# A decode kernel whose value, key and output-weight loads move from SyncE's DMA queue to GpSimd's, each engine's share in one packet

## The chip, the cores and the metric

The kernel runs on one core of a Trainium2 chip. The metric is the device time of one execution, in microseconds (us). A core has TensorE (PE), VectorE (DVE), ScalarE (ACT), GpSimd (POOL) and SyncE (SP), which run their own instruction streams and meet at semaphores, and 16 DMA engines that move data between the chip's memory (HBM) and the core's on-chip memory of 128 partitions. A DMA is issued by one of the engines, goes into that engine's queue, and is spread over the 16 DMA engines; each of them adds 1 to the DMA's semaphore when its share has landed, so a finished DMA counts 16.

## What is computed

One token of a gated mix of two parts. Nearly all the work is in the first, attention over a cache of 65536 positions with 8 key/value heads of size 256 and 16 query heads:

```python
q = (x @ wq).reshape(B, Sq, Hq, Dh)           # 1 token, Hq = 16, Dh = 256
k = jnp.repeat(k_cache, 2, axis=1)            # k_cache, v_cache: 1 x 8 x 65536 x 256, bf16
scores = jnp.einsum("bhqd,bhkd->bhqk", q, k) * (Dh ** -0.5)
o = jnp.einsum("bhqk,bhkd->bhqd", softmax(scores), v)
a = o.reshape(B, Sq, Hq * Dh) @ wo
out = g * a + (1 - g) * b                     # g = sigmoid(sum(x * gate_w)); b: a small MLP of x
```

The two caches are 256 MB each; the weights W_q and W_o are under 4 MB each. The second part, b, is a LayerNorm and an MLP along the token axis, done on DVE and ACT in small pieces beside the attention.

## The kernel before

The cache of one head is read in 4 pieces, so that there are 32 *bodies* (j = 0 to 31) of 16384 positions, each with 8 MB of keys and 8 MB of values. A body is a tile of 128 partitions with 128 positions each, 64 KB per partition. Keys go to `kring` (L107), which has room for one and a half bodies; values go to `vbuf` (L109), which has room for one. `vbuf` holds W_q and the small inputs at the start.

PE works through a body in 8 *chunks* of 16 positions per partition. For each it transposes the keys through the identity (`transposes`, L344 to L370, the matmul of L359), DVE and ACT copy the result to `ktT` (L675, L820), and PE multiplies it with the query (`scores`, L380). Chunks 0 to 3 use positions 64 to 127 of the body, chunks 4 to 7 positions 0 to 63. After the last chunk the running maximum is updated (`maxima`), ACT makes the weights `pT` (L807), and PE multiplies them with the values (`values`, L411 within `some`). For bodies 0 and 1 the values follow the keys of the same body. From body 3 on (`LEAD` = 2) PE first does the keys of body j and then the values of body j - 1. At the end of a head, PE projects the result with a piece of W_o (`wo_rows`, L466 to L472, the wait in L574).

All large loads are issued by SP, in the order of its program (L257 to L323):

- The first piece of W_o (L263), W_q in two parts (L264, L266), and the keys of body 0 in two halves, positions 64 to 127 first (L272), then 0 to 63 (L273). None of them waits.
- `load_v(j)` (L275 to L285) loads the values of body j: for j = 0 after W_q has been used (`s_q`, `s_hb`), otherwise after the values of body j - 1 have been used (`sem_pv`). At the first body of a head it also loads the next piece of W_o.
- The loop of L287 to L308 loads the keys of body j after PE has transposed chunk 3 of body j - 1 (L294; the semaphore of bank 3 counts chunks), then the values of body j, for j of 2 and less, or of body j - 1. Body 2 comes in two halves, body 3 in a half and two quarters, body 31 in two halves.
- The values of body 31 come in five pieces (L311 to L316), the last piece of W_o in two (L317 to L320), and at the end SP stores the output (L322).

All these loads of whole key bodies count on one semaphore, `sem_k`, for which PE waits before chunk 0 (L346) with 16 x (j + 1). The second halves have their own semaphores, for which PE waits before chunk 4 (L347 to L351). The two quarters of body 3 have two semaphores of their own; POOL waits for both and then adds 16 to `sem_k` (L335 to L337). This, and the making of an identity matrix and of ones at the start (L327 to L334), is all that POOL does. ACT issues six small loads at the start (L780 to L785).

Of the kernel before, what the change touches and what calls it, by code (L numbers as in the profile page):

```python
# [7 lines left out]
AF = mybir.ActivationFunctionType  # L8
ALU = mybir.AluOpType
AX = mybir.AxisListType  # L10


def bass_gated_mix__gqa_block_cached__mixer_token_mlp__decode_kernel(
# [17 lines left out]
    H = A_k_cache.shape[1]  # L31
    T = A_k_cache.shape[2]
    DH = A_k_cache.shape[3]
    DM = A_x.shape[-1]
    HQ = A_wq.shape[1] // DH
    REP = HQ // H
# [9 lines left out]
    DC = 4  # L46
    NB = NT // 4
    NCPH = T // CH
    NC = H * NCPH
    BODY = 2 * DC  # L50
    NV = BODY * NT
    NP = NC // BODY
    PPH = NCPH // BODY
# [10 lines left out]
    LEAD = 2  # L64
    assert LEAD % 2 == 0 and 1 < LEAD < PPH
    NLATE = 112
    NRING = 72
    pieces = [(0, NRING), (NRING, 96), (96, NLATE), (NLATE, 124), (124, NV)]
# [16 lines left out]
    HV = NV // 2  # L85
# [11 lines left out]
    with ctx:  # L97
# [6 lines left out]
        def new_sem(name):  # L104
            return ctx.enter_context(nc.semaphore(name))

        kring = sb([P, NV + HV, DH], bf16, "kring")  # L107
        kring_f = kring.bitcast(f32)
        vbuf = sb([P, NV, DH], bf16, "vbuf")  # L109
# [10 lines left out]
        wo_sb = sb([P, REP, 2 * DM], bf16, "wo_sb")  # L120


        wo_rows = wo_sb[:, :, :].rearrange("p h n -> p (h n)")
# [73 lines left out]

        sem_k = new_sem("sem_k")
        sem_kb = new_sem("sem_kb")
        sem_kc = [new_sem("sem_kc%d" % i) for i in range(3)]  # L200
        sem_kq = [new_sem("sem_kq%d" % i) for i in range(2)]
        sem_v = new_sem("sem_v")
        sem_vp = [new_sem("semvp%d" % i) for i in range(len(pieces))]
# [3 lines left out]
        sem_wo = new_sem("sem_wo")  # L207
# [6 lines left out]
        sem_pv = new_sem("sem_pv")  # L214
# [37 lines left out]
        def src(cache, j, n0=0, n1=NV):  # L252
            g, m = divmod(j, PPH)
            s = cache[0, g, m * BODY * CH:(m + 1) * BODY * CH, :].rearrange("(p n) d -> p n d", p=P)
            return s[:, n0:n1, :].rearrange("p n d -> p (n d)")

        @block.sync  # L257
        def _(eng):
            def load_wo(g):
                w = A_wo[g * REP * DH:(g + 1) * REP * DH, :]  # L260
                eng.dma_start(wo_rows, w.rearrange("(p i) n -> p (i n)", i=2 * REP)).then_inc(sem_wo, 16)

            load_wo(0)  # L263
            eng.dma_start(wq_a.rearrange("p j n -> p (j n)"),  # L264
                          A_wq[0:WF * P, :].rearrange("(p j) n -> p (j n)", p=P)).then_inc(sem_wq, 16)
            eng.dma_start(wq_b, A_wq[WF * P:DM, :].rearrange("r (a n) -> (r a) n", a=2)  # L266
                          ).then_inc(sem_wq, 16)
            def load(dst, cache, j, n0, n1, at, sem):
                eng.dma_start(dst[:, at + n0:at + n1, :].rearrange("p n d -> p (n d)"), src(cache, j, n0, n1)
                              ).then_inc(sem, 16)  # L270

            load(kring, A_k_cache, 0, HV, NV, 0, sem_k)  # L272
            load(kring, A_k_cache, 0, 0, HV, 0, sem_kb)  # L273

            def load_v(j):  # L275
                if j == 0:
                    eng.wait_ge(s_q, 1)
                    eng.wait_ge(s_hb, 1)
                else:
                    eng.wait_ge(sem_pv, j)  # L280
                load(vbuf, A_v_cache, j, 0, NV, 0, sem_v)
                g, m = divmod(j, PPH)
                if m == 0 and 1 <= g < H - 1:
                    eng.wait_ge(s_proj, g)
                    load_wo(g)  # L285

            for j in range(NP):  # L287
                if j == LEAD + 1:
                    eng.wait_ge(sem_tr[NB - 1], BODY * LEAD)
                    load(kring, A_k_cache, j, HV, NV, HV, sem_kc[1])  # L290
                    eng.wait_ge(sem_tr[NB - 1], BODY * LEAD + DC // 2)
                    load(kring, A_k_cache, j, 0, HV // 2, HV, sem_kq[0])
                if j >= 1:
                    eng.wait_ge(sem_tr[NB - 1], BODY * (j - 1) + DC)  # L294
                if j == LEAD:
                    load(kring, A_k_cache, j, HV, NV, 0, sem_k)
                    load(kring, A_k_cache, j, 0, HV, 0, sem_kc[0])
                elif j == LEAD + 1:
                    load(kring, A_k_cache, j, HV // 2, HV, HV, sem_kq[1])
                elif j == NP - 1:  # L300
                    load(kring, A_k_cache, j, 0, HV, HV, sem_k)
                    load(kring, A_k_cache, j, HV, NV, HV, sem_kc[2])
                elif j >= 1:
                    load(kring, A_k_cache, j, 0, NV, HV * (j % 2), sem_k)
                if j < LEAD:
                    load_v(j)
                elif j > LEAD:
                    load_v(j - 1)  # L308


            for (n0, n1), sem in zip(pieces, sem_vp):  # L311
                if n0 == 0:
                    eng.wait_ge(sem_tr[NB - 1], BODY * (NP - 1) + DC)
                elif n0 == NRING:
                    eng.wait_ge(sem_pv, NP - 1)
                load(kring if n1 <= NRING else vbuf, A_v_cache, NP - 1, n0, n1, 0, sem)  # L316
            eng.wait_ge(s_proj, H - 1)  # L317
            for h in range(REP):
                w = A_wo[(HQ - REP + h) * DH:(HQ - REP + h + 1) * DH, :]
                eng.dma_start(wo_sb[:, h, :], w.rearrange("(p j) n -> p (j n)", j=2)).then_inc(sem_wl[h], 16)  # L320
            eng.wait_ge(s_fin, NCG)
            eng.dma_start(out_ap, out_row[:, :]).then_inc(sem_out, 16)  # L322
            eng.wait_ge(sem_out, 16)  # L323

        @block.gpsimd
        def _(eng):
            eng.memset(ident[:, :], 0.0)  # L327
            eng.drain()
            eng.affine_select(
                out=ident[:, :], in_=ident[:, :], compare_op=ALU.not_equal, fill=1.0,  # L330
                base=0, pattern=[[-1, P]], channel_multiplier=1,
            )
            eng.drain()
            eng.memset(ones_sq[:, :], 1.0).then_inc(sem_ident, 1)  # L334
            for sem in sem_kq:  # L335
                eng.wait_ge(sem, 16)
            eng.sem_inc(sem_k, 16)  # L337

        @block.tensor
        def _(pe):  # L340
# [2 lines left out]

            def transposes(k, c, j, u16, x2):  # L344
                if k == 0:
                    pe.wait_ge(sem_k, u16)  # L346
                if k == DC:  # L347
                    pe.wait_ge(sem_kb, 16)
                    for p, sem in zip((LEAD, LEAD + 1, NP - 1), sem_kc):
                        with pe.If(j == p):  # L350
                            pe.wait_ge(sem, 16)  # L351

                done = pe.snap(c + 1, min_val=1, max_val=NC)

                def tiles(at):
                    for b in range(NB):
                        pe.wait_ge(sem_ev[b], done)
                        for i in range(4):
                            ins = pe.transpose(kst[:, b, i * P:(i + 1) * P],  # L359
                                               kring_f[:, at + NT * (k % DC) + 4 * b + i, :], ident[:, :])  # L360
                        ins.then_inc(sem_tr[b], 1)

                if k < DC:
                    tiles(HV)
                else:
                    with pe.If(x2 == 0):
                        tiles(0)
                    with pe.Else():
                        tiles(NV)
# [165 lines left out]
            pe.reg_mov(m_reg, 0)  # L535
            g_reg = pe.alloc_register("g_reg")
            pe.reg_mov(g_reg, 1)
            with nc.Fori(0, NP + 1, 1, engines=on, head_slot={pe.engine: 0}) as jj:
                j = pe.snap(jj, min_val=0, max_val=NP)
                m = pe.snap(m_reg, min_val=0, max_val=PPH)  # L540
# [4 lines left out]
                    maxima(pe.snap(j, min_val=1, max_val=NP))  # L545
                with pe.If(j < NP):
                    c0 = pe.snap(j * BODY, min_val=0, max_val=NC)
                    u16 = pe.snap(j * 16 + 16, min_val=16, max_val=16 * NP)
                    keys(c0, j, u16, pe.snap(x2_reg, min_val=0, max_val=NV))
                with pe.Else():  # L550
                    pe.wait_ge(s_mix, 1)
# [16 lines left out]
                with pe.If(m >= PPH):  # L568
                    with pe.If(j < NP):
                        g1 = pe.snap(g - 1, min_val=1, max_val=H)  # L570
                        pe.wait_ge(s_cp, g1)
                        clear(acc[:, 0:NACC])
                        by_row(acc[:, SELC:NACC]).then_inc(s_sel, 1)
                        pe.wait_ge(sem_wo, pe.snap(g * 16 - 16, min_val=16, max_val=16 * H))  # L574
                        pe.wait_ge(s_oTn, g1)
                        project(range(2 * REP)).then_inc(s_proj, 1)
                        pe.reg_mov(m_reg, 0)
# [281 lines left out]
```

## Time and profile before

| | |
|---|---|
| time, median of 3 runs | 1264.36 us (1263.95 to 1264.56) |
| span of the profiled execution, first to last instruction | 1262.8 us |
| HBM read | 544.22 MB, 431 GB/s over the span |
| PE busy | 974.4 us (77%) |
| DVE busy | 498.3 us (39%) |
| ACT busy | 545.7 us (43%) |
| POOL busy | 0.9 us |
| DMA issues by SP | 7 of W_o with 448 KB, 31 of values and 28 of keys with 8 MB, and the halves and pieces |

The profiled execution is known by its span; the time of a run has what lies around the span in it, and the median of the runs is 1.56 us above this span. Times inside the profile count from the span's start. "Busy" leaves out waiting, branching and the issuing of DMAs. A row such as `19.55 0.33 SPq L269 DMA_DIRECT2D vbuf<-in_A_v_cache_dram` is an issue: at 19.55 us, 0.33 us long, on SP's queue, by line 269, of a load into `vbuf`. In brackets stands how long an engine was idle before an instruction, and what ended it. In the rows of DMA queues the numbers are packets, MB, and the time that the packets took as a share of the time of 16 DMA engines; in those of issues, the size of one and the median us from issue to landing.

### The profile page before, as it was taken

What the parts mean: (1) busy time and instruction counts of PE and PEld (TensorE: products, weight loads), DVE (VectorE), ACT (ScalarE), POOL (GpSimd) and SP (SyncE); (2) the same over time, 40 slices, a digit from 0 to 9 for tenths busy, and PEclk for the clock granted to TensorE, in tenths of its full rate; (3) what the DMA queues carried; (4) which work ended last, traced back from release to release, by engine and by line L of the source; (5) the groups of instructions that cost most, each with busy time, mean ns of one, the idle gap of its engine ahead of it and who ended that gap; (6) DMA issues with size and microseconds to landing.
All of it is one profiled execution on the core that took longest, in us unless ns stands there. A gap on an engine that the chain in (4) does not pass through costs nothing.

```text
span 1262.8 us, 39606 instructions
## 1 busy us (share of the span) xinstructions
PE 974.4 (77%) x17019; PEld 891.1 (71%) x17019; DVE 498.3 (39%) x1126; ACT 545.7 (43%) x692; POOL 0.9 (0%) x7
## 2 busy tenths in 40 slices
PE   4768887678777797776977678886778866798787
PEld 3667876678667687666877667876668766687685
DVE  3234434344444435444354433342333432334342
ACT  2344643345433455343454334443344433445352
POOL 0000000000000000000000000000000000000000
PEclk8878888898877888788888889887798877888787
DMA  9999999999999999999999999999999999999998
GB/s 415 433 421 426 439 436 436 432 432 432 432 434 440 436 432 432 432 430 438 434 434 429 437 434 432 432 432 436 436 436 432 432 432 432 432 434 438 428 438 370
DMA packets 12197, 544.35 MB, mean 431 GB/s; under 512 B 1433, under 2 KB 1692, under 8 KB 2972
## 3 DMA queue, kind: packets, MB, share of 16 engines
q1 hardware_dynamic: 12098, 544.22, 99.8%
q8 instruction: 6, 0.10, 0.0%
q10 hardware_dynamic: 90, 0.01, 0.0%
q14 instruction: 3, 0.02, 0.0%
HBM read 544.22 MB, written 0.00 MB: 431 GB/s over the span
## 4 chain that ended last, share of the span: by engine, by line
DMA 58%; PE 37%; DVE 2%; issue 2%; DVEq 0%; SPq 0%; ACT 0%
DMA kring<-in_A_k_cache_dram 55%; PE kst L359 26%; PE sps L380 6%; PE acc L411 3%; DMA vbuf<-in_A_v_cache_dram 2%; DMA wo_sb<-in_A_wo_dram 1%; PE acc L461 0%; PE sps L399 0%; PE prj L472 0%; DVE ktT L675 0%; ACT z_b L825 0%; PE acc L404 0%; DVE accs L709 0%; PE sps L397 0%; DVE mrow L686 0%
## 5 line engine op out<-in xcount | busy, mean ns | idle before, releaser
L359 PE MATMUL kst<-ident,kring 128*128 128x128 f32 x4096 | 565.0, 299 | 181.4 <-DMA kring<-in_A_k_cache_dram 158.2
L359 PEld LDWEIGHTS kst<-ident,kring 128*128 128x128 f32 x4096 | 513.1, 156 | 190.7 <-issue 184.6
L820 ACT ACTIVATE ktT<-kst 128x1024 bf16<-128x1024 bf16 x512 | 499.9, 1021 | 337.2 <-PE kst L359 336.8
L675 DVE COPY ktT<-kst 128x1024 bf16<-128x1024 bf16 x512 | 353.9, 692 | 435.5 <-PE kst L359 409.4
L380 PEld LDWEIGHTS sps<-qcur,ktT 128*128 128x128 bf16 x8192 | 238.0, 97 | 2.6
L380 PE MATMUL sps<-qcur,ktT 128*128 128x2 bf16 x8192 | 236.6, 163 | 0.0
L411 PE MATMUL acc<-vbuf,pT 128*2 128x256 bf16 x4008 | 164.1, 341 | 4.6 <-issue 3.3
L411 PEld LDWEIGHTS acc<-vbuf,pT 128*2 128x2 bf16 x4008 | 113.5, 103 | 47.0 <-issue 4.5
L803 ACT ACTIVATE fade<-mdif 128x2 f32<-128x2 f32 x32 | 6.5, 203 | 305.1 <-DVE mdif L692 305.1
L686 DVE TENSOR_REDUCE mrow<-sps 2x1 f32<-2x128 f32 x32 | 8.9, 279 | 162.6 <-PE sps L397 162.6
L399 PEld LDWEIGHTS sps<-mdiag,mones 2*128 2x128 f32 x64 | 11.1, 216 | 27.9 <-DVE mdiag L688 27.9
L397 PE MATMUL sps<-ident,mcol 128*2 128x128 f32 x32 | 8.9, 279 | 27.9 <-issue 26.4
L399 PE MATMUL sps<-mdiag,mones 2*128 2x2 f32 x64 | 13.9, 284 | 21.3 <-DVE mdiag L688 21.3
L807 ACT ACTIVATE pT<-sps,mneg 128x64 f32 x128 | 30.3, 334 | 0.0
L825 ACT ACTIVATE z_b<-z_b 128x448 bf16<-128x448 bf16 x14 | 8.1, 576 | 48.2 <-DVE z_b L662 48.2
L404 PE MATMUL acc<-pT,ones_sq 128*128 128x32 bf16 x256 | 12.0, 182 | 21.9 <-issue 18.4
L397 PEld LDWEIGHTS sps<-ident,mcol 128*2 128x2 f32 x32 | 2.6, 80 | 36.6 <-issue 28.3
L709 DVE COPY accs<-acc 128x288 f32<-128x288 f32 x8 | 3.7, 458 | 61.7 <-PE acc L411 61.7
L681 DVE TENSOR_REDUCE mcol<-sps 128x2 f32<-128x256 f32 x32 | 13.5, 423 | 34.6 <-PE sps L380 34.6
L404 PEld LDWEIGHTS acc<-pT,ones_sq 128*128 128x128 bf16 x256 | 8.8, 99 | 26.0 <-issue 22.4
L704 DVE TENSOR_SCALAR acc<-acc,fader 128x256 f32<-128x256 f32 x32 | 15.8, 493 | 2.5
L691 DVE TENSOR_SCALAR mneg<-sps 128x2 f32<-128x2 f32 x32 | 5.1, 160 | 16.8 <-PE sps L399 16.8
(113 smaller groups left out, 168.8 us busy)
## 6 DMA issues: line engine op xcount, KB each, us to landing
kring<-in_A_k_cache_dram SPq DMA_DIRECT2D x7, 4096.0 KB, 25.2
kring<-in_A_v_cache_dram SPq DMA_DIRECT2D x1, 4608.0 KB, 25.4
kring<-in_A_k_cache_dram SPq DMA_DIRECT2D x2, 2048.0 KB, 13.1
wo_sb<-in_A_wo_dram SPq DMA_DIRECT2D x7, 448.0 KB, 25.3
vbuf<-in_A_wq_dram SPq DMA_DIRECT2D x1, 3072.0 KB, 10.8
vbuf<-in_A_v_cache_dram SPq DMA_DIRECT2D x1, 1536.0 KB, 8.1
vbuf<-in_A_v_cache_dram SPq DMA_DIRECT2D x1, 1024.0 KB, 10.2
vbuf<-in_A_v_cache_dram SPq DMA_DIRECT2D x1, 768.0 KB, 11.6
```

The lines of the kernel that those rows point to most:

```text
L359: ins = pe.transpose(kst[:, b, i * P:(i + 1) * P], kring_f[:, at + NT * (k % DC) + 4 * b + i, :], ident[:, :])
L380: ins = pe.matmul(sps[:, 0, 2 * (NT * k + nt):2 * (NT * k + nt) + 2], ktT[:, par, b, ntl * DH + dj:(ntl + 1) * DH:2], qcur[:, dj, :], star ...
L397: pe.transpose(mxT, mcol[:, :], ident[:, :]).then_inc(s_mT, 1)
L399: pe.matmul(mxB, mones[:, :], mdiag[:, :], start=True, stop=True).then_inc(s_mB, 1)
L404: pe.matmul(acc[:, DENC:SELC], ones_sq[:, :], pT[:, r, :], start=False, stop=(r == BODY - 1), skip_group_check=True)
L411: ins = pe.matmul(acc[o:o + REP, 0:DH], pT[:, r, 2 * nt:2 * nt + 2], buf[:, n, :], start=False, stop=False, skip_group_check=True)
L675: vec.tensor_copy(ktT[:, k % KTB, b, :], kst_b[:, b, :]).then_inc(sem_ev[b], 1)
L681: vec.tensor_reduce(out=mcol[:, :], in_=scores_all.rearrange("p (n hh) -> p hh n", hh=REP), axis=AX.X, op=ALU.max)
L686: vec.tensor_reduce(out=mrow[:, :], in_=mxT, axis=AX.X, op=ALU.max)
L704: vec.tensor_scalar(acc[:, 0:DENC], acc[:, 0:DENC], fader[:, :], None, op0=ALU.mult).then_inc(s_acc, 1)
L807: ins = act.activation(pT[:, bass.ds(p0, DC), hh:2 * NT:REP], scores_all.rearrange("p (a r n hh) -> p a hh r n", a=2, r=DC, hh=REP)[:, hal ...
L820: act.activation(ktT[:, k % KTB, b, :], kst_b[:, b, :], AF.Copy).then_inc(sem_ev[b], 1)
```

## The change

SP keeps the first piece of W_o, W_q, the two halves of the keys of body 0, and the store of the output. All other loads, beginning with the values of body 0, are issued by POOL, in the same order and with the same waits, and with the option `single_packet`, which puts all descriptors that a DMA engine has of one load into one packet. (A descriptor moves one contiguous run, here a row of one partition.)

The semaphores follow: the keys of body 0 and the first piece of W_o get their own (`sem_k0`, `sem_wo0`), so that each counts loads of one queue only. Since POOL's program now holds the loads, the wait for the two quarters of body 3 moves from POOL to PE, and PE counts with registers what it has to wait for.

```diff
+HOW = {"single_packet": True}
...
+        def load(eng, dst, cache, j, n0, n1, at, sem, **how):
+            eng.dma_start(dst[:, at + n0:at + n1, :].rearrange("p n d -> p (n d)"), src(cache, j, n0, n1), **how
+                          ).then_inc(sem, 16)
...
         @block.sync
...
-            load(kring, A_k_cache, 0, HV, NV, 0, sem_k)
-            load(kring, A_k_cache, 0, 0, HV, 0, sem_kb)
+            load(eng, kring, A_k_cache, 0, HV, NV, 0, sem_k0)
+            load(eng, kring, A_k_cache, 0, 0, HV, 0, sem_kb)
             eng.wait_ge(s_fin, NCG)
             eng.dma_start(out_ap, out_row[:, :]).then_inc(sem_out, 16)
...
         @block.gpsimd
...
             eng.memset(ones_sq[:, :], 1.0).then_inc(sem_ident, 1)
-            for sem in sem_kq:
-                eng.wait_ge(sem, 16)
-            eng.sem_inc(sem_k, 16)
+            how = dict(HOW)
+
+            def load_v(j):
+                if j == 0:
+                    eng.wait_ge(s_q, 1)
+                    eng.wait_ge(s_hb, 1)
+                else:
+                    eng.wait_ge(sem_pv, j)
+                load(eng, vbuf, A_v_cache, j, 0, NV, 0, sem_v, **how)
...
+            for j in range(NP):
...
+                if j >= 1:
+                    eng.wait_ge(sem_tr[NB - 1], BODY * (j - 1) + DC)
...
+                elif j >= 1:
+                    load(eng, kring, A_k_cache, j, 0, NV, HV * (j % 2), sem_k, **how)
...
                 if k == 0:
-                    pe.wait_ge(sem_k, u16)
+                    with pe.If(j == LEAD + 1):
+                        for sem in sem_kq:
+                            pe.wait_ge(sem, 16)
+                    with pe.Else():
+                        with pe.If(j > 0):
+                            pe.wait_ge(sem_k, u16)
+                            pe.reg_add(u_reg, u_reg, 16)
+                        with pe.Else():
+                            pe.wait_ge(sem_k0, 16)
...
-                        pe.wait_ge(sem_wo, pe.snap(g * 16 - 16, min_val=16, max_val=16 * H))
+                        with pe.If(g > 2):
+                            pe.wait_ge(sem_wo, pe.snap(w_reg, min_val=16, max_val=16 * H))
+                            pe.reg_add(w_reg, w_reg, 16)
+                        with pe.Else():
+                            pe.wait_ge(sem_wo0, 16)
```

More of the change, by code (lines that the diff above doesn't have):

```diff
@@ L199, in bass_gated_mix__gqa_block_cached__mixer_token_mlp__decode_kernel @@
         sem_kb = new_sem("sem_kb")
+        sem_k0 = new_sem("sem_k0")
+        sem_wo0 = new_sem("sem_wo0")
         sem_kc = [new_sem("sem_kc%d" % i) for i in range(3)]
@@ L255, in src, with load_wo @@
             return s[:, n0:n1, :].rearrange("p n d -> p (n d)")
+        def load(eng, dst, cache, j, n0, n1, at, sem, **how):
+            eng.dma_start(dst[:, at + n0:at + n1, :].rearrange("p n d -> p (n d)"), src(cache, j, n0, n1), **how
+                          ).then_inc(sem, 16)
+        def load_wo(eng, g, **how):
+            w = A_wo[g * REP * DH:(g + 1) * REP * DH, :]
+            eng.dma_start(wo_rows, w.rearrange("(p i) n -> p (i n)", i=2 * REP), **how).then_inc(sem_wo, 16)
         @block.sync
         def _(eng):
[L259 to L263, printed above, removed]
+            eng.dma_start(wo_rows, A_wo[0:REP * DH, :].rearrange("(p i) n -> p (i n)", i=2 * REP)
+                          ).then_inc(sem_wo0, 16)
             eng.dma_start(wq_a.rearrange("p j n -> p (j n)"),
@@ L267, in _ @@
                           ).then_inc(sem_wq, 16)
-            def load(dst, cache, j, n0, n1, at, sem):
-                eng.dma_start(dst[:, at + n0:at + n1, :].rearrange("p n d -> p (n d)"), src(cache, j, n0, n1)
-                              ).then_inc(sem, 16)
-            load(kring, A_k_cache, 0, HV, NV, 0, sem_k)
-            load(kring, A_k_cache, 0, 0, HV, 0, sem_kb)
[L275 to L308, printed above, removed]
@@ L311, in _ @@
[L311 to L320, printed above, removed]
+            load(eng, kring, A_k_cache, 0, HV, NV, 0, sem_k0)
@@ L334, in _ @@
             eng.memset(ones_sq[:, :], 1.0).then_inc(sem_ident, 1)
-            for sem in sem_kq:
-                eng.wait_ge(sem, 16)
-            eng.sem_inc(sem_k, 16)
+            how = dict(HOW)
[6 more added lines that the diff above has]
+                load(eng, vbuf, A_v_cache, j, 0, NV, 0, sem_v, **how)
+                g, m = divmod(j, PPH)
+                if m == 0 and 1 <= g < H - 1:
+                    eng.wait_ge(s_proj, g)
+                    load_wo(eng, g, **how)
@@ new lines, in _ @@
+            for j in range(NP):
+                if j == LEAD + 1:
+                    eng.wait_ge(sem_tr[NB - 1], BODY * LEAD)
+                    load(eng, kring, A_k_cache, j, HV, NV, HV, sem_kc[1], **how)
+                    eng.wait_ge(sem_tr[NB - 1], BODY * LEAD + DC // 2)
+                    load(eng, kring, A_k_cache, j, 0, HV // 2, HV, sem_kq[0], **how)
+                if j >= 1:
+                    eng.wait_ge(sem_tr[NB - 1], BODY * (j - 1) + DC)
+                if j == LEAD:
+                    load(eng, kring, A_k_cache, j, HV, NV, 0, sem_k, **how)
+                    load(eng, kring, A_k_cache, j, 0, HV, 0, sem_kc[0], **how)
+                elif j == LEAD + 1:
+                    load(eng, kring, A_k_cache, j, HV // 2, HV, HV, sem_kq[1], **how)
+                elif j == NP - 1:
+                    load(eng, kring, A_k_cache, j, 0, HV, HV, sem_k, **how)
+                    load(eng, kring, A_k_cache, j, HV, NV, HV, sem_kc[2], **how)
+                elif j >= 1:
+                    load(eng, kring, A_k_cache, j, 0, NV, HV * (j % 2), sem_k, **how)
+                if j < LEAD:
+                    load_v(j)
+                elif j > LEAD:
+                    load_v(j - 1)
@@ new lines, in _ @@
+            for (n0, n1), sem in zip(pieces, sem_vp):
+                if n0 == 0:
+                    eng.wait_ge(sem_tr[NB - 1], BODY * (NP - 1) + DC)
+                elif n0 == NRING:
+                    eng.wait_ge(sem_pv, NP - 1)
+                load(eng, kring if n1 <= NRING else vbuf, A_v_cache, NP - 1, n0, n1, 0, sem, **how)
+            eng.wait_ge(s_proj, H - 1)
+            for h in range(REP):
+                w = A_wo[(HQ - REP + h) * DH:(HQ - REP + h + 1) * DH, :]
+                eng.dma_start(wo_sb[:, h, :], w.rearrange("(p j) n -> p (j n)", j=2), **how
+                              ).then_inc(sem_wl[h], 16)
@@ L537, in _ @@
             pe.reg_mov(g_reg, 1)
+            u_reg = pe.alloc_register("u_reg")
+            pe.reg_mov(u_reg, 16)
+            w_reg = pe.alloc_register("w_reg")
+            pe.reg_mov(w_reg, 16)
             with nc.Fori(0, NP + 1, 1, engines=on, head_slot={pe.engine: 0}) as jj:
@@ L547, in _ @@
                     c0 = pe.snap(j * BODY, min_val=0, max_val=NC)
-                    u16 = pe.snap(j * 16 + 16, min_val=16, max_val=16 * NP)
+                    u16 = pe.snap(u_reg, min_val=16, max_val=16 * NP)
                     keys(c0, j, u16, pe.snap(x2_reg, min_val=0, max_val=NV))
```

## The prediction

> **What bounds the kernel now.** I read the page's DMA rows first, then the DMA view of two windows, then the chain.
>
> ```profile
> DMA  9999999999999999999999999999999999999998
> ...
> q1 hardware_dynamic: 12098, 544.22, 99.8%
> ...
> q10 hardware_dynamic: 90, 0.01, 0.0%
> ```
>
> The first row is the DMA busy share in 40 slices, the second SP's queue: 12098 packets, 544.22 MB, and its packets took 99.8% of what 16 engines had; the third is ACT's. No compute engine matters as long as this holds: the span is bytes over rate. So the change can act in two ways only: through the time of a packet, and through stretches in which the engines have nothing to do. For the first, one window with large packets (260 to 1190 us) and one with small ones (1250 to 1260):
>
> ```profile
> q1 hardware_dynamic: 7605, 403.18, 100.2%
> ```
> ```profile
> q1 hardware_dynamic: 835, 3.94, 95.7%
> ```
>
> The large one is 930 us x 16 x 1.002 = 14909 engine-us, the small one 10 x 16 x 0.957 = 153.1. With a cost c per packet and a rate r per engine: 14909 = 7605c + 403.18 MB/r and 153.1 = 835c + 3.94 MB/r. This gives c = 9.7 ns and r = 27.2 GB/s. So a load of 8 MB (8 packets of 64 KB on each engine, and one for the semaphore) takes 19.3 us at 434 GB/s, and only 0.09 us of that are costs per packet. For the second I read the chain, in steady state and at the start (start us, us, what):
>
> ```profile
> 2.13 20.62 DMA kring<-in_A_k_cache_dram
> ...
> 22.88 5.85 PE kst L359 x32
> ...
> 33.93 38.45 DMA kring<-in_A_k_cache_dram
> ...
> 72.51 6.62 PE kst L359 x32
> ...
> 259.11 27.43 DMA kring<-in_A_k_cache_dram
> ```
>
> In steady state a load lands 27.4 us after its issue and needs 19.3: it stood about **8 us behind the load before it**. A later start of up to 8 us costs nothing there. At the start, the first half of keys (K0a, positions 64 to 127 of body 0) lands at 22.75, and the keys of body 1 (K1), issued at 33.93, at 72.38.
>
> **The change, part by part.**
>
> *The packets.* Of 12098 packets, SP keeps those of its first five loads, 5 x (128 + 16) = 720. The other 11378 are 711 per engine, or 711 x 9.7 ns = 6.9 us. If the cost is one of a packet and 9 become one, 8/9 of this goes: 6.1 us. If it is one of a descriptor, nothing goes. No row separates the two; I take the middle, **3 us gained** (0 to 6.9). [...]
>
> *The issue.* Nothing in the trace is issued by POOL's queue, so the delay d from the end of POOL's wait to the first byte is bounded by rows of SP and ACT:
>
> ```profile
> 19.55 0.33 SPq L269 DMA_DIRECT2D vbuf<-in_A_v_cache_dram  x1
> 33.93 0.33 SPq L269 DMA_DIRECT2D kring<-in_A_k_cache_dram  x1
> ...
> 63.02 0.33 SPq L269 DMA_DIRECT2D vbuf<-in_A_v_cache_dram  x1
> 84.33 33.70 SPq L269 DMA_DIRECT2D kring<-in_A_k_cache_dram  x5
> ...
> 1225.62 0.33 SPq L269 DMA_DIRECT2D kring<-in_A_v_cache_dram  x1
> 1246.66 1.75 SPq L269 DMA_DIRECT2D vbuf<-in_A_v_cache_dram  x4
> 1248.45 0.90 SPq L320 DMA_DIRECT2D wo_sb<-in_A_wo_dram  x2
> ```
> ```profile
> 0.73 0.53 ACTq L780 DMA_DIRECT2D vbuf<-in_A_x_dram  x1
> ...
> 2.13 0.22 PE L492 MATMUL acc<-ones_sq,vbuf 1*128 1x1 bf16 x3 [2.13 <-DMA vbuf<-in_A_x_dram]
> ...
> 2.85 0.32 ACTq L785 DMA_DIRECT2D b_b<-in_B_b_dram  x1
> ...
> 11.81 0.38 DVE L616 TENSOR_TENSOR vbuf<-vbuf 1x448 bf16<-1x448 bf16 x1 [5.80 <-DMA b_b<-in_B_b_dram]
> ```
> ```profile
> wo_sb<-in_A_wo_dram SPq DMA_DIRECT2D x1, 448.0 KB, 3.2
> ```
>
> It is at least one issue on SP, 0.33 us, and at most the whole life of the first load of 448 KB, 3.2. I take **1.4 us**, the life of the one-row load of x (0.73 to 2.13), the nearest row to a load that finds its path free. [...] In steady state d lies under the 8 us of cover. Each K load keeps its place ahead of the V load on POOL's queue, and the same waits stand before them, so what is queued behind a waiting issue is what was queued behind it on SP. In the tail six loads go out from 1246.66, while V's first piece, behind the values that PE takes up at about 1240, has some 11 us (4.5 MB) to run, to 1251; then follow 9.8 us of data. Six issues of 1.4 us end at 1255, before the last of them is due: nothing. At 3.2 us each they would add some 5 us.
>
> *PE.* Two or three branches at the first chunk of a body, and the wait for the two quarters of body 3 that POOL did before.
>
> ```profile
> 35.16 1.96 PE L359 MATMUL kst<-ident,kring 128*128 128x128 f32 x16 [0.48 <-issue]
> ```
> ```profile
> PE kst L359 <- DMA kring<-in_A_k_cache_dram: 158.2, 29, 9.5
> ```
>
> The branches at the fifth chunk show as 0.48 us of "issue"; before the keys, PE waits 158.2 / 29 = 5.5 us a time for DMA. Costed at nothing; without this cover it would be 32 x 0.5 = 16 us.
>
> *Two rings.* This is what decides. Until now K0a, K0b (positions 0 to 63) and V0 stood in one ring, in order. Now V0 comes on another ring while K0a and K0b are still under way, and the 16 engines are the same. How an engine chooses between rings is seen at the start: the 2-byte load of b2, issued by ACT at 2.85, is what DVE still waited for at 11.81. ACT's loads are some 10 KB; ahead of SP's they would have landed soon, behind all of them after 30 us. What fits is a turn for each ring: six ACT loads on one engine are 12 packets (data and semaphore), x's two were through at 2.13, and ten turns beside W_q's packets of 24 KB (24576 B / 27.2 GB/s = 0.90 us) give 2.13 + 9.0 = 11.1. [...]
>
> With V0's share as **one packet of 512 KB per engine**, a turn of POOL's ring lasts 19.3 us. POOL's waits end at 19.55, the packet is there at 20.95, and K0a is due at 22.75: its last descriptors or its semaphore packets stand behind V0. Two rows more, PE's first values of body 0 and V1's landing:
>
> ```profile
> 52.99 4.43 PE L411 MATMUL acc<-vbuf,pT 128*2 128x256 bf16 x77 [0.50 <-DMA vbuf<-in_A_v_cache_dram]
> ```
> ```profile
> vbuf<-in_A_v_cache_dram SPq DMA_DIRECT2D x1, 28.7
> ```
>
> - K0a lands at 22.75 + 19.3 = 42.1; K0b (4 MB, 9.7 us) at 51.7, in time for PE's fifth chunk at 35.16 + 19.3 = 54.5.
> - K1 is issued at 33.93 + 19.3 = 53.2, on its ring at 54.6, landed at 73.9: the engines were empty for up to 3 us.
> - V1 needs PE to finish the values of body 0: 63.02 + 19.3 = 82.3, less the 0.5 us that PE waited for V0 = 81.8. Its bytes run from 83.2, some 9 us after K1 landed, and land at 102.5. Before, V1 landed 28.7 us after 63.02, at 91.7. **The transfers are 10.8 us late.**
> - PE starts body 1's keys some 10 to 11 us late too, so K2 goes out at about 95 instead of 84.33, 7 us ahead of V1's landing. The cover is back, nothing else is lost, and nothing is regained, since the engines are full from here on.
>
> **Sum:** 10.8 - 3.0 = +7.8 us. The profiled execution's 1262.8 becomes 1270.6; the three runs' median is 1.56 above that span, so 1264.36 + 7.8 = **1272.2 us**. Its own range: d from 0.33 to 3.2 moves the 10.8 to 9.7 to 12.6, the packets take 6.9 to 0 off: 1267 to 1277.
>
> **The rivals.**
>
> *A: V0 comes later than K0a's end*, d over 3.2 us. K0a lands in time, but K0b's 8 descriptors then get one turn between V0's packet and K1's (issued at 33.93): 22.75 + 19.3 + 19.3 + 9.7 = 71 instead of 32.4. PE's fifth chunk waits until then, 36 us late; V1 goes out at 99, runs from 102 and lands at 121.6, 30 late: 1291 with the gain. Against it: d would have to be twice what I take; for it: no row has POOL's d.
>
> *B: the packets aren't joined*, each descriptor its own turn, and the change does not do what it says. K0a is 2.4 to 4.8 us late; K0b's 8 turns of 1.2 us alternate with 64 KB of V0 and K1 (2.4 us): about 58. V1 goes out at 86, 23 late, runs from 87 and lands at 106.6, 15 late, with no gain: 1279.
>
> *C: no turn is lost*, since the engines finish what SP's ring holds (its descriptors already fetched) before the new packet. Then V0 and K1 keep their times, d is hidden, and the gain stands alone: 1264.4 - 3 = 1261.4, from 1257.5 (all of the packet cost) to 1264.4. Against it speaks b2 at 11.81; for it, that no row here shows a large packet against SP's ring.
>
> [...]
>
> **How the numbers follow.** Forecast 0.45; A 0.16; B 0.08; C 0.26; D 0.05. A measurement of this kernel tells about 0.2% (2.5 us) from no change. C is faster where over 2.5 us are gained, two thirds of it: faster 0.17, same 0.09; all else is slower: 0.74. The range takes in the forecast, B, A with d a little over its bound, and the upper half of C: 1260 to 1293; left out are the large gains of C (0.1) and D.
>
> **What would show it.** Right: the first transposes start at about 42 us instead of 22.88; the DMA row has slices under 9 around 52 and 74 to 83 us, and none later; the steady rate is up by a few tenths of a per cent, or the packets of POOL's queue are fewer or shorter. A shows as a first transposes' start at 22.9 and PE without work from 34 to 71; B as a start at 25 to 28; C as 22.9 with K0b in time. The prediction is wrong at its root if K0a and K0b land when they did.

## The result and the profile after

The changed kernel takes 1273.36 us (median of 4 runs, 1272.02 to 1274.51), the kernel before 1264.46 us in the same comparison: a ratio of 1.0069, 95% interval 1.0055 to 1.0084, or 8.9 us more. The prediction was 1272.2 us, slower. The time and the place of the loss came as forecast; the way there did not, as the rows show.

The page of the changed kernel, with the span, the DMA busy tenths of 40 slices, and the queues (q0 is POOL's):

```profile
span 1271.0 us, 39745 instructions
...
DMA  9979999999999999999999999999999999999998
...
q0 software_dynamic: 10768, 531.70, 96.8%
q1 hardware_dynamic: 722, 12.52, 2.3%
```

One slice of 40 is under 9, besides the last, which reads 8 before the change too: the third, 64 to 95 us. To see how much is lost there, compare what had been moved after 100 us, and the steady part; first the kernel before, then the changed one:

```profile
DMA packets 1396, 42.30 MB, mean 423 GB/s; under 512 B 225, under 2 KB 227, under 8 KB 483
```
```profile
DMA packets 1282, 38.84 MB, mean 388 GB/s; under 512 B 216, under 2 KB 218, under 8 KB 474
...
q0 software_dynamic: 7283, 403.05, 100.1%
```

The last row is the window of 260 to 1190 us, and answers to 7605 packets, 403.18 MB, 100.2% of before: the same bytes in the same time, to 0.3 us. In the first 100 us 3.46 MB fewer were moved, which at 434 GB/s is 8.0 us. The spans differ by 8.2. So in this trace the whole loss, to some tenths of a us, lies at the start. The chain, PE's first transposes of the halves and bodies, and POOL's issues tell what happened:

```profile
2.60 47.94 DMA kring<-in_A_k_cache_dram
50.54 1.06 issue
51.60 3.48 PE kst L370 x16
```
```profile
23.01 5.85 PE L370 MATMUL kst<-ident,kring 128*128 128x128 f32 x32 [3.48 <-DMA kring<-in_A_k_cache_dram]
...
51.60 3.48 PE L370 MATMUL kst<-ident,kring 128*128 128x128 f32 x16 [16.79 <-issue]
...
79.98 6.36 PE L370 MATMUL kst<-ident,kring 128*128 128x128 f32 x32 [3.77 <-issue]
```
```profile
19.76 0.68 POOL L262 DMA_DIRECT2D vbuf<-in_A_v_cache_dram  x1 [17.93 <-DVE hbT L763]
34.35 0.53 POOL L262 DMA_DIRECT2D kring<-in_A_k_cache_dram  x1 [13.91 <-PE kst L370]
76.53 0.53 POOL L262 DMA_DIRECT2D vbuf<-in_A_v_cache_dram  x1 [41.66 <-PE acc L422]
```

K0a came in time: PE starts at 23.01 (22.88 before). K0b came at 50.54 instead of about 33.4 (before, it landed 30.8 us after its issue at about 2.6): the fifth chunk starts at 51.60 instead of 35.16, and the 16.79 us ahead of it are put down to "issue", though by the chain it was the load. After this wait the chunk's 16 transposes take 3.48 us, before 1.96. K1 was issued about when it was before (34.35, before 33.93). But V1 waits for the values of body 0, which need K0b: it goes out at 76.53 instead of 63.02, after K1 has landed (38.0 us after its issue, at 72.4). In the view by windows (PE, PEld, DVE, ACT, POOL, granted clock, DMA share, GB/s; a packet counts where it begins), before and after:

```profile
72.00:80.00 8.00, 7.49 (x66) 7.48 (x67) 2.77 (x4) 3.91 (x4) 0.00 (x0) 0.59 1.04 451
```
```profile
73.00:74.00 1.00, 1.00 (x24) 0.69 (x20) 0.00 (x0) 0.00 (x0) 0.00 (x0) 0.50 0.00 0
...
76.00:77.00 1.00, 0.22 (x8) 0.00 (x0) 0.00 (x0) 0.00 (x0) 0.47 (x1) 1.00 0.00 0
...
72.00:80.00 8.00, 4.23 (x97) 2.69 (x89) 0.00 (x0) 0.00 (x0) 0.53 (x1) 0.71 0.40 133
```

From K1's landing to V1's first packets, at 77.7, the DMA engines stand all but empty: first while PE multiplies body 0's values, to 76.22, then while POOL's issue takes effect.

The order on the engines is seen in the packets of both queues from 26 to 46 us, while K0b (32 KB each) and V0 (64 KB each) are both under way:

```profile
q0 software_dynamic: 87, 5.70, 66.1%
q1 hardware_dynamic: 94, 3.08, 35.7%
```

As many packets of the one as of the other, and twice the bytes. Short windows of the same trace show the order, for all 16 engines together:

| us | packets of V0 that begin | packets of K0b that begin |
|---|---|---|
| 24 to 25.5 | 15 | 0 |
| 26 to 27.5 | 0 | 15 |
| 27.5 to 29.5 | 16 | 1 |
| 30 to 31 | 0 | 15 |
| 31 to 32 | 15 | 1 |

So it is **one descriptor of each ring in turn** in this trace, although V0's descriptors were to form one packet.

### The profile page after: what moved, and what is told of

Read it like the earlier page. It is cut to its first block, busy times and chain, and to the rows that moved or that the text cites. A ratio compares the mean times of both kernels' runs of the same rounds, so it can differ in the third digit from the quotient of the medians.

```text
span 1271.0 us, 39745 instructions
## 1 busy us (share of the span) xinstructions
PE 960.4 (76%) x17019; PEld 881.5 (69%) x17019; DVE 498.2 (39%) x1126; ACT 544.6 (43%) x692; POOL 42.8 (3%) x86
## 4 chain that ended last, share of the span: by engine, by line
DMA 60%; PE 35%; issue 3%; DVE 1%; DVEq 0%; POOL 0%; SPq 0%; ACT 0%
DMA kring<-in_A_k_cache_dram 57%; PE kst L370 25%; PE sps L391 6%; PE acc L422 3%; DMA vbuf<-in_A_v_cache_dram 2%; DMA wo_sb<-in_A_wo_dram 1%; PE acc L472 0%; PE sps L410 0%; POOL vbuf L262 0%; PE acc L415 0%; PE prj L483 0%; PE sps L408 0%; DVE ktT L694 0%; DVE mrow L705 0%; DVE mcol L700 0%
## 5 line engine op out<-in xcount | busy, mean ns | idle before, releaser
L370 PE MATMUL kst<-ident,kring 128*128 128x128 f32 x4096 | 557.2, 297 | 206.7 <-DMA kring<-in_A_k_cache_dram 163.6
L370 PEld LDWEIGHTS kst<-ident,kring 128*128 128x128 f32 x4096 | 506.3, 154 | 214.2 <-issue 210.6
L422 PE MATMUL acc<-vbuf,pT 128*2 128x256 bf16 x4008 | 159.3, 334 | 3.0 <-DMA vbuf<-in_A_v_cache_dram 3.0
L262 POOL DMA_DIRECT2D vbuf<-in_A_v_cache_dram x35 | 18.6, 532 | 592.6 <-PE acc L422 574.6
L262 POOL DMA_DIRECT2D kring<-in_A_k_cache_dram x35 | 18.5, 528 | 592.0 <-PE kst L370 592.0
```

The costliest lines, as they stand in the source:

```text
L370: ins = pe.transpose(kst[:, b, i * P:(i + 1) * P], kring_f[:, at + NT * (k % DC) + 4 * b + i, :], ident[:, :])
L422: ins = pe.matmul(acc[o:o + REP, 0:DH], pT[:, r, 2 * nt:2 * nt + 2], buf[:, n, :], start=False, stop=False, skip_group_check=True)
```

## The experiments

The theory after this comparison: an engine gives each ring one descriptor in turn, whatever its size and whether or not it is joined to others, and the loss is K0b's wait behind V0's descriptors, nothing else. Rivals: joined packets matter; POOL's loads are slower by themselves; PE's new branches cost time. The diffs are against the changed kernel; ratios are against the kernel before, with their 95% interval.

### Is it the joined packet?

```diff
-HOW = {"single_packet": True}
+HOW = {}
```

> Theory (turns by descriptor: an engine gives each ring one descriptor in turn, whether or not its descriptors are joined, and the key half K0b stands between the descriptors of V0): without the option the time is that of the changed kernel, 1273.4 us within 2 us, K0b and V0 alternate as before, and a 64 KB packet takes the same time. Rival (turns by packet: the joined packets matter): without them V0 gives way to K0b more often or the packets take longer; the time leaves 1273.4 by over 2.5 us, upwards by up to 6 us if joining saved the cost per packet.

Measured: 1272.65 us, 1.0068 (1.0055 to 1.0082). The packets from 26 to 46 us:

```profile
q0 software_dynamic: 90, 5.90, 68.4%
q1 hardware_dynamic: 94, 3.08, 35.7%
```

The same turns, and a median within 1 us of the changed kernel's. The option has no effect here that these runs can tell: 1272.65 us without it, 1273.36 with it. No run shows that it puts the descriptors of a load into one packet; whether it joins nothing, or an engine leaves a joined packet after each descriptor, they don't tell either. (Packets do get fewer on POOL's queue, 7283 for 7605 from 260 to 1190 us, but these are W_o's, 64 a load instead of 128, with the option on and off.)

The same question on SP's queue, with the loop of loads moved back into SP's program, with the option off (`HOW = {}`, as above) and on. The edit moves the head of POOL's program behind the loop, which so becomes a part of SP's:

```diff
             load(eng, kring, A_k_cache, 0, 0, HV, 0, sem_kb)
-            eng.wait_ge(s_fin, NCG)
...
-        @block.gpsimd
-        def _(eng):
...
             how = dict(HOW)
...
+            eng.wait_ge(s_fin, NCG)
...
+        @block.gpsimd
+        def _(eng):
```

> The changed kernel with all loads issued by SP again and the option off; what is left of the change are the semaphores and the branches on PE. Theory: 1264.5 within 1.5 us. Rival (the branches or the counting on PE cost time): 1267 or more.

> All loads issued by SP, with the option on for all but its first five. Theory (the cost per packet is one of a descriptor and joining saves nothing): 1264.5 within 1.5 us. Rival (joining saves up to 8/9 of 6.9 us, the estimate of the prediction): 1258 to 1262.

Measured: 1264.48 us, 1.0004 (0.9995 to 1.0013) without, 1264.71, 1.0003 (0.9994 to 1.0012) with the option. So the semaphores and PE's branches cost nothing that can be told from zero, and the option saves nothing. The steady window (260 to 1190) with the option on SP:

```profile
q1 hardware_dynamic: 7602, 402.98, 100.1%
```

The trace of the first of these runs, with the option off on POOL's queue, also shows a second part of the loss. It is of that run's longest execution, 1275.67 us. Of the 14 executions of the changed kernel, of that run and of the one below with an earlier first load on POOL's queue, 9 took 1271.5 to 1272.7 us and 5 took 1274.4 to 1275.7. The difference lies in the same stretch. The sixth chunk of body 0 and V1's issue, in the changed kernel's trace (1272.29 us) and in that one:

```profile
55.72 1.95 PE L370 MATMUL kst<-ident,kring 128*128 128x128 f32 x16
```
```profile
56.09 3.65 PE L370 MATMUL kst<-ident,kring 128*128 128x128 f32 x16
...
79.15 0.53 POOL L262 DMA_DIRECT2D vbuf<-in_A_v_cache_dram  x1 [44.69 <-PE acc L422]
```

In the changed kernel's trace the granted clock was 0.50 from 50 to 54 us, after PE's wait for K0b, 0.63 in the next us, and 1.00 from 55 to 64 us; one chunk was slow, with 3.48 us for its transposes. In the longer execution three were, at 51.73, 56.09 and 60.44, with 3.67, 3.65 and 3.65 us, and the fourth took 1.95 again. V1 went out 2.6 us later, and after 100 us another 1.01 MB were missing (37.83 for 38.84), or 2.3 us. Why three chunks were slow there and not one is not shown, and only one trace is of the longer kind.

### Is it the two rings, or POOL?

K0b goes into POOL's ring, ahead of V0:

```diff
@@ sync
-            load(eng, kring, A_k_cache, 0, 0, HV, 0, sem_kb)
@@ gpsimd, load_v(0)
                     eng.wait_ge(s_q, 1)
+                    load(eng, kring, A_k_cache, 0, 0, HV, 0, sem_kb, **how)
                     eng.wait_ge(s_hb, 1)
```

> K0b, the second half of body 0's keys, is issued by POOL too, once W_q has been used, so that it stands ahead of V0 in the same ring. Theory (the loss comes only from two rings that share the engines while K0b is under way): K0b lands near 33 us instead of 51, the values of body 1 go out near 63 instead of 76.5, and the time is 1264.5 within 2 us. Rival (POOL's loads themselves are slower, a little at each of some 65 loads): the time stays above 1269.

Measured: 1265.1 us, 1.0007 (0.9997 to 1.0016), no difference from before, though 98% of the packet time is POOL's:

```profile
q0 software_dynamic: 10912, 535.89, 98.2%
q1 hardware_dynamic: 578, 8.32, 1.6%
```
```profile
36.30 1.96 PE L370 MATMUL kst<-ident,kring 128*128 128x128 f32 x16 [0.52 <-issue]
```
```profile
17.04 0.67 POOL L262 DMA_DIRECT2D kring<-in_A_k_cache_dram  x1 [15.21 <-PE kst L518]
19.43 0.53 POOL L262 DMA_DIRECT2D vbuf<-in_A_v_cache_dram  x1 [1.73 <-DVE hbT L763]
...
64.19 0.53 POOL L262 DMA_DIRECT2D vbuf<-in_A_v_cache_dram  x1 [28.36 <-PE acc L422]
```

The fifth chunk starts at 36.30 and V1 goes out at 64.19, ahead of K1's landing. K0a, the last load in SP's ring here, lands 21.5 us after its issue instead of 20.6, and PE starts at 23.98 instead of 22.88; a turn of POOL's ring ahead of K0a's semaphore packets would fit, but no row shows which packets came between. The time doesn't show it. In this kernel, where a load is issued some 8 us ahead of its turn, POOL's loads are as good as SP's (1.0007) when the ring holds them in the right order. This undoes the loss and keeps the change; it isn't faster than the kernel before.

The other way to keep the rings apart is to let POOL wait:

```diff
                     eng.wait_ge(s_hb, 1)
+                    eng.wait_ge(sem_kb, 16)
```

> POOL waits until K0b has landed before it issues V0; all else as changed. Theory (two rings on the same engines are the whole loss): K0b lands near 33 us; the engines are then empty for the delay of POOL's issue, 1.6 to 4.6 us, and this is all that is lost: 1266 to 1269.5 us. Rival (POOL's loads themselves are slower): over 1271.

Measured: 1269.67 us, 1.0043 (1.0029 to 1.0056), 5.3 us lost, just above what was expected. POOL's issue, the first packets of its queue from 34.1 to 35.5 us and to 36, and the windows row of 22 to 34 us (before: DMA share 1.07, 458 GB/s):

```profile
34.10 0.67 POOL L262 DMA_DIRECT2D vbuf<-in_A_v_cache_dram  x1 [32.27 <-DMA kring<-in_A_k_cache_dram]
```
```profile
q0 software_dynamic: 1, 0.07, 12.9%
...
q0 software_dynamic: 12, 0.79, 118.6%
```
```profile
22.00:34.00 12.00, 11.27 (x141) 11.24 (x142) 5.39 (x8) 6.85 (x8) 0.00 (x0) 0.78 0.73 309
```

From POOL's issue to the first bytes it took 1.4 to 1.9 us here, on 12 of the 16 engines, with empty engines; V1 of the changed kernel, issued at 76.53, has the first packets of all 16 engines between 77.7 and 78.2, 1.2 to 1.7 us after. The rest of the 5.3 fits with engines that end K0b at different times and stand empty until the last has landed, since POOL's wait is released only then: from 31 to 33.5 us hardly a data packet begins (0.08 MB).

### The size of the descriptors

If turns go by descriptor, K0b's landing must follow the sizes. V0 in two loads (32 KB descriptors) and in four (16 KB), with a semaphore of their own for all but the last; and K0b in two loads (16 KB) beside V0 unchanged:

```diff
-                load(eng, vbuf, A_v_cache, j, 0, NV, 0, sem_v, **how)
+                if j == 0:
+                    load(eng, vbuf, A_v_cache, j, 0, HV, 0, sem_v0, **how)
+                    load(eng, vbuf, A_v_cache, j, HV, NV, 0, sem_v, **how)
+                else:
+                    load(eng, vbuf, A_v_cache, j, 0, NV, 0, sem_v, **how)
```
```diff
+                    for n in range(0, NV, 32):
+                        load(eng, vbuf, A_v_cache, j, n, n + 32, 0, sem_v if n == 96 else sem_v0, **how)
```
```diff
-            load(eng, kring, A_k_cache, 0, 0, HV, 0, sem_kb)
+            load(eng, kring, A_k_cache, 0, 0, HV // 2, 0, sem_kb)
+            load(eng, kring, A_k_cache, 0, HV // 2, HV, 0, sem_kb)
```

> The values of body 0 come as two loads of 32 KB descriptors (positions 0 to 63 and 64 to 127) with two semaphores, all else as changed. Theory (turns by descriptor): K0b's 8 descriptors of 32 KB alternate with 32 KB instead of 64 KB, so K0b lands about 8 x 1.2 = 9.7 us sooner, near 42 us instead of 51; the values of body 1 go out near 67 to 70 us, before the keys of body 1 have landed, and the time is 1264 to 1267 us. Rival (one ring is served before the other, or the two share by time and not by descriptor): K0b still lands near 51 and the time stays near 1273.

> The values of body 0 come as four loads of 16 KB descriptors; all else as changed. Theory: K0b's descriptors alternate with 16 KB, so it lands near 24 + 6 x 1.8 + 1.2 = 36 to 39 us, 12 to 15 us sooner than with 64 KB; the values of body 1 go out near 66 to 69, and the time is 1264.5 to 1267 us, below the 1268.8 of the halves. Rival (the halves won for another reason, such as their semaphores): 1268 to 1273.

> K0b comes as two loads of 16 KB descriptors, still issued by SP; all else as changed. Theory (a ring gets one descriptor in turn, whatever its size): two of K0b's 16 descriptors go first, then each waits for a 64 KB descriptor of V0 or K1, 14 x (0.6 + 2.4) = 42 us: K0b lands near 65 us instead of 50.5, the values of body 1 go out near 90, and the time is 1284 to 1290 us. V0's first bytes come about 1.2 us sooner if two descriptors of SP's ring go ahead of them, whatever their size. Rival (the rings share by time or by bytes): K0b lands near 50, time 1272 to 1274.

Measured: halves 1268.8 us, 1.0039 (1.0025 to 1.0053); quarters 1266.91 us, 1.0018 (1.0009 to 1.0027); K0b's quarters 1289.72 us, 1.0212 (1.0197 to 1.0226). The start of the fifth chunk, and V1's issue, of the three in this order:

```profile
43.19 3.67 PE L375 MATMUL kst<-ident,kring 128*128 128x128 f32 x16 [8.75 <-issue]
...
71.67 0.53 POOL L263 DMA_DIRECT2D vbuf<-in_A_v_cache_dram  x1 [37.18 <-PE acc L427]
```
```profile
38.73 3.47 PE L375 MATMUL kst<-ident,kring 128*128 128x128 f32 x16 [3.67 <-issue]
...
68.94 0.53 POOL L263 DMA_DIRECT2D vbuf<-in_A_v_cache_dram  x1 [33.83 <-PE acc L427]
```
```profile
67.65 3.67 PE L371 MATMUL kst<-ident,kring 128*128 128x128 f32 x16 [32.17 <-issue]
...
92.72 0.53 POOL L262 DMA_DIRECT2D vbuf<-in_A_v_cache_dram  x1 [57.18 <-PE acc L423]
```

| V0's descriptors / K0b's | K0b's fifth chunk | V1's issue | ratio |
|---|---|---|---|
| not beside each other (one ring) | 36.30 | 64.19 | 1.0007 |
| 16 KB / 32 KB | 38.73 | 68.94 | 1.0018 |
| 32 KB / 32 KB | 43.19 | 71.67 | 1.0039 |
| 64 KB / 32 KB (the change) | 51.60 | 76.53 | 1.0069 |
| 64 KB / 16 KB | 67.65 | 92.72 | 1.0212 |

The arithmetic holds for all four to 1 us. With V0 on the engines from about 24.3 (below) and two of K0b's descriptors gone before it, six turns of 1.2 + 2.4 us and one before the semaphore's packet make 24.1 us: 48.4. (In the rows of 26 to 46 us a packet of 32 KB takes 1.22 us and one of 64 KB 2.43; for 16 KB half of the former, 0.6, is an estimate.) In the trace the 16 packets of V0 that follow K0b's last data begin between 45.5 and 48 us; 14 of the 16 semaphore packets begin between 48 and 49.5 us and the last two after 50, so the last engine is some 2 us later, and PE starts 1.1 us after that: 51.5 for the measured 51.60. With 32 KB it is 24.3 + 6 x 2.4 + 1.2, or 39.9, with 16 KB 24.3 + 6 x 1.8 + 0.6, or 35.7; with the same 3.1 us behind, 43.0 and 38.8 for 43.19 and 38.73. K0b's quarters have 12 turns of 0.6 + 2.4 and two semaphore packets with 2.4 ahead of each: 65.3, and 68.4 for 67.65. Smaller descriptors of K0b made it *later*, 67.65 for 51.60: SP's ring got 16 KB of it in a turn beside V0's 64 KB, instead of 32 KB. The halves came out 1.8 us above the expected range, since V1's issue at 71.67 was later than the 67 to 70 that was expected (the fifth chunk took 3.67 us instead of 1.96). K1 landed at 72.5, too close for a POOL issue to be hidden: in that trace the engines moved 7 GB/s from 70 to 72.5 us, at a busy share under a tenth.

### Why V0 came as late as it did

V0 was issued at 19.76, and the windows of 20 to 24 and 20 to 24.5 us of the changed kernel show when its packets begin:

```profile
q1 hardware_dynamic: 64, 1.57, 91.2%
q0 software_dynamic: 1, 0.07, 3.8%
...
q0 software_dynamic: 14, 0.92, 47.0%
```

Over 4 us after the issue, where 1.2 to 1.9 were seen with empty engines. One cause to try is that it is the first load of POOL's queue:

```diff
             how = dict(HOW)
+            eng.dma_start(warm[:, :], A_k_cache[0, 0, 0:P, 0:16], **how).then_inc(sem_warm, 16)
+            eng.wait_ge(sem_warm, 16)
```

> POOL issues a tiny load of 128 rows of 32 bytes into an unused tile at the start and waits for it; all else as changed. First-use theory (the first load of POOL's queue starts 3 us later than its others, since something is fetched for it): V0's first bytes come about 3 us sooner, so that its descriptors take turns with the last of K0a: the first transposes start at 25 to 28 us instead of 23.0, K0b lands within 1.5 us of 51, and the time is within 2.5 us of 1273.4. Rival (descriptors of SP's ring that an engine has already taken up come first): V0 starts when it did, the first transposes at 23.0, time 1273.4 within 1 us.

Measured: 1272.33 us, 1.0067 (1.0053 to 1.0081). V0, issued at 19.91, starts no sooner; 20 to 24 and 20 to 24.5 us:

```profile
q1 hardware_dynamic: 64, 1.57, 91.2%
...
q0 software_dynamic: 14, 0.92, 47.0%
```

So it isn't the first use. The run with K0b's quarters speaks on the rival, that two descriptors of SP's ring go first. Its V0 was issued at 20.09:

```profile
q1 hardware_dynamic: 94, 1.57, 91.6%
q1 hardware_dynamic: 96, 1.61, 83.1%
q0 software_dynamic: 13, 0.85, 43.7%
```

Again nothing of POOL's by 24.0 and 13 packets by 24.5, but now 96 packets of SP's from 20 to 24.5 instead of 64: K0a's last and its semaphore (32), and four of 16 KB on each engine instead of two of 32 KB. It isn't a number of descriptors, and the expected 1.2 us didn't come. With V0 in quarters it was the same: issued at 19.59, it has no packet by 23.5 us, 2 by 24.0 and 15 by 24.5. Whether it is an amount of bytes already taken up, or a time that POOL's path needs beside a busy ring, these runs don't separate; this stays open.

## Why the prediction was right, and where its steps were not

- **What bounds the kernel: right.** The engines' rate is the same to 0.1% in the steady part, and the loss is a stretch without transfers, 3.46 MB or 8.0 us of the 8.2.
- **Two rings are what decides: right.** With K0b and V0 in one ring the loss is gone (1.0007).
- **The turn of a ring is a whole joined packet: wrong.** It is one descriptor, with the option on or off. The prediction drew this from b2's small packets, where both readings are the same, and named the other reading as a rival (B, 0.08). That a turn lasts for the whole of a joined packet, 19.3 us, was the author's estimate, and no run shows such a turn. What the runs showed in its place are 87 descriptors of 64 KB beside 94 of 32 KB in 20 us with the option on, 90 beside 94 with it off.
- **d = 1.4 us: right for empty engines (1.2 to 1.9), wrong for V0**, over 4 us, beyond the bound of 3.2 taken from the nearest rows. So V0 missed K0a (23.01 instead of the forecast 42), and none of the cases was met as drawn: it was B's turns with A's late V0.
- **K0b at 51.7: 50.54.** Nearly the same number by another way, and that is luck: K0b and V0 have 8 descriptors each on an engine, so that taking turns they end about together, and K0b lands about where it would behind all of V0. With other sizes it lands elsewhere (the table above), which the prediction's way does not give. This is why the sum was close: V1 waits for K0b.
- **V1 issued at 81.8: 76.53.** PE had done its first four chunks before, so only the second half was late, and the fifth chunk started at 51.60 and not at 54.5. From there to V1's issue it took 24.9 us, before 27.9: the chunk itself was slower (3.48 us for 1.96), but PE did the values without the 3.29 us of idle time that stood among them before. The transfers were 8.0 us late and not 10.8.
- **3 us gained on packets: 0.** Of the bounds 0 and 6.9 the lower one holds, on both queues. The cost per packet was worked out from two windows, an estimate; either it is one of a descriptor, or the option joins nothing, and in both cases there was nothing to gain.
- **The sum:** 10.8 - 3.0 = 7.8 forecast, 8.0 - 0 in the trace, 8.9 (7.0 to 10.6) in the runs. Two terms were off by about 3 us each, in opposite directions; that the sum is so near is luck. The median of the runs lies above the trace, since two of the four are of the longer kind.
- **Steady cover, PE's branches and the tail at nothing: right.** POOL's issues of 0.53 us instead of SP's 0.33 vanish under the cover, and loads in SP's ring with the new branches take 1.0004.

## What to carry to other kernels

Before loads move to another engine's queue, look for transfers of the old queue that are still under way at the first issue. Here the order that one ring had kept was lost at that point: K0b, needed first, shared the engines with V0, needed later, descriptor by descriptor, and PE's fifth chunk started at 51.60 instead of 35.16. Keeping both in one ring, in the order of need, gave 1.0007 instead of 1.0069. Where two rings had to share in these runs, the one with the smaller descriptors got fewer bytes (3.08 MB beside 5.70). And with the engines full from there on (434 GB/s from 260 to 1190 us before, 433 after), the 8.0 us lost at the start were not made up later.

## What the runs showed of the hardware

- Turns between two rings went by descriptor: 64 KB beside 32 KB gave 5.70 MB beside 3.08 MB in 20 us. The semaphore's packets waited for a turn too: the last 16 packets of V0 ahead of K0b's semaphore begin between 45.5 and 48 us in the changed kernel's trace, the 16 semaphore packets between 48 and 50.5, one descriptor of 64 KB (2.43 us) later.
- POOL's queue carries these loads at the rate of SP's (403.05 against 403.18 MB in 930 us), beside DVE's 498 us of work in the whole execution.
- Its first bytes came 1.2 to 1.9 us after an issue to empty engines (V1 on all 16 engines, and V0 on 12 of them in the run in which POOL waits for K0b), and 4.0 to 4.7 us after V0's issue beside SP's ring in use (the first packet between 23.75 and 24.0 us, 14 of 16 by 24.5).
- `single_packet` changed nothing that could be measured, on either queue: 1.0069 with it and 1.0068 without on POOL's, 1.0003 and 1.0004 on SP's.
- After a wait of PE of 3.67 us or more before the fifth chunk of a body (least with V0 in quarters, 38.73), the chunk's 16 transposes took 3.47 to 3.67 us, after one of 0.64 us or less 1.96. In the changed kernel's trace the granted clock was 0.50 from 50 to 54 us, around such a chunk. In one execution three of them came in a row, with 3.65 to 3.67 us each, and V1 went out 2.6 us later.
